# A fused recurrent attention and ELU feed-forward kernel: the lead-in, the conversion of float64 weights and the spacing of two products rearranged

**Chip, cores, metric.** One core of one Trainium2 chip. The metric is the time of one execution on the device in microseconds (us), the median of several. TensorE is called PE, its weight loads PEld, VectorE DVE, ScalarE ACT, GpSimd POOL, SyncE SP.

## The reference

A recurrent attention (per head a 48 x 48 state, decayed and updated at each step) gives x with 3072 tokens of 384 features. A feed-forward layer with ELU follows. The two weight matrices come as float64.

```python
# q, k, v, f_logit: (4 batches, 8 heads, 768 steps, 48), float32
f = 1 / (1 + exp(-f_logit))
for t in range(768):
    state = f[:, :, t, :, None] * state + einsum('bhd,bhe->bhde', k[:, :, t], v[:, :, t])
    y[:, :, t] = einsum('bhd,bhde->bhe', q[:, :, t], state)
x = y as (3072, 384)
h = x @ w_in                    # w_in  384 x 2048, float64 in DRAM
g = where(h > 0, h, exp(min(h, 0)) - 1)
out = g @ w_out                 # w_out 2048 x 384, float64 in DRAM
```

## The kernel before

The tokens go in 12 units of 256. In block m the kernel does the feed-forward layer of unit m and, in between, the attention of unit m + 1. A block has 16 places s. At even places stands an *up* product (a pair of feature tiles: 12 matmuls into `psH`), whose result goes through ACT (relu, exp) and DVE (`gg`); at odd places a *down* product of an earlier pair. `xt` is a unit's attention output, turned so that the up product can read it; `wi` (three rows kt of 2048 columns) and `wo` are the converted weights.

```python
def up(P):                                   # pair P = 8 m + j
    ph = ps.tile([128, 2, U], FP32, tag="h", bufs=2)
    for i in range(2):
        for kt in range(3):
            matmul(ph[:, i], lhsT=wi[:, kt, n : n + 128], rhs=xts[m][:, kt, :], ...)
    g = gs[P] = sb.tile([128, 2, U], FP32, tag="gg", bufs=4)
    scalar.activation(g, ph, Relu, scale=-1.0);  scalar.activation(g, g, Exp, scale=-1.0)
    vector.scalar_tensor_tensor(out=g, in0=g, scalar=-1.0, in1=ph, op0=add, op1=max)
    # ... from block 2 on: 4 sums of g for the product scheme with seven products

def attention(u):                            # places at which the pieces of unit u stand
    return {3: [transposed(u, 0), transposed(u, 1)],   # psT: k transposed
            6: [advance(u)],                 # psU: state products, then the state steps on DVE
            8: [scores(u)],                  # psS: scores, in the same two PSUM banks as psU
            10: [outputs(u)], 12: [carried(u)]}        # psY
```

A float64 word is read as two 32-bit words and rounded to float32 on the chip, 16 parts of 768 KB, all in block 0 and just before it:

```python
def rounding(n):   # ACT, in place: low word -> 0..8
    scalar.activation(raw.bitcast(I32)[:, 0::2], raw.bitcast(U32)[:, 0::2], Copy, scale=2.0**-29)
def convert(n):    # three DVE instructions
    tensor_scalar(out=bits, in0=hi, scalar1=3, scalar2=0x3FFFFFF8, op0=logical_shift_left, op1=bitwise_and)
    tensor_tensor(out=bits, in0=bits, in1=rnd, op=add)
    scalar_tensor_tensor(out=to, in0=hi, scalar=-(2**30), in1=bits, op0=bitwise_and, op1=bitwise_or)
```

The instructions of block 0 and of the lead-in keep the order of the source; after that the build's scheduler sets the order of every engine. 16 *checks* read the weights a second time and reduce them (32 reductions on DVE), to see that all lie in the range that the conversion supports. Unit 0 has code of its own before: its outputs are multiplied straight into the places of `xt` that the up product reads, while for all other units six small DMA moves inside `xt` put a part of the rows in place.

Of the kernel before, what the change touches and what calls it, by code (L numbers as in the profile page):

```python
# [8 lines left out]
FP32 = mybir.dt.float32  # L9
I32 = mybir.dt.int32  # L10
U32 = mybir.dt.uint32
AF = mybir.ActivationFunctionType
# [343 lines left out]
def fast(ctx: ExitStack, tc: tile.TileContext, q, k, v, f_logit, w_in, w_out, out, flag):  # L356
# [14 lines left out]

# [17 lines left out]
    DIRECT = 2  # L389
    AHEAD = 7  # L390
# [35 lines left out]
    start.enter_context(tc.manual_schedule())  # L426
    blank(0, nc.vector, nc.gpsimd)
    load(0, nc.scalar)

    ident = cst.tile([128, 128], FP32, name="ident")  # L430
# [14 lines left out]
    for i in range(1, NB):  # L445
        blank(i, nc.gpsimd)
    between = cst.tile([128, NW, HP], FP32, name="between")
    fine = cst.tile([128, HP, NC], FP32, name="fine")
    nc.vector.memset(fine[:], 1.0)
    py = ps.tile([128, HP, W], FP32, tag="a1", name="psY")  # L450
    nc.vector.memset(py[:], 0.0)
# [15 lines left out]
    parts = [(0, 0), *((j + i, 1 - i) for j in range(NFT // 2 - 1) for i in (1, 0)), (NFT // 2 - 1, 1)]  # L467
# [19 lines left out]
    def rounding(n):  # L487

        if wide and n < NFT:
            raw = raws[n]  # L490
            nc.scalar.activation(
                raw.bitcast(I32)[:, 0::2], raw.bitcast(U32)[:, 0::2], AF.Copy, scale=2.0**-29
            )

    def convert(n):





        if not wide or n >= NFT:
            return
        j, out_ = parts[n]
        raw = raws.pop(n)
        rnd = raw.bitcast(I32)[:, 0::2]
        hi = raw.bitcast(I32)[:, 1::2]
        bits = sb.tile([128, 2 * DM], I32, tag="bits", name=f"bits{n}", bufs=1)
        nc.vector.tensor_scalar(
            out=bits[:], in0=hi, scalar1=3, scalar2=0x3FFFFFF8,
            op0=ALU.logical_shift_left, op1=ALU.bitwise_and,  # L510
        )
        nc.vector.tensor_tensor(out=bits[:], in0=bits[:], in1=rnd, op=ALU.add)
        to = wo[:, 2 * j : 2 * j + 2] if out_ else wi[:, :, j * 256 : (j + 1) * 256]

        def rows(x):
            return x.rearrange("p (k f) -> p k f", k=to.shape[1])

        nc.vector.scalar_tensor_tensor(
            out=to.bitcast(I32), in0=rows(hi), scalar=-(2**30), in1=rows(bits[:]),
            op0=ALU.bitwise_and, op1=ALU.bitwise_or,  # L520
        )
# [19 lines left out]

    restart = cst.tile([128, HP, U], FP32, name="restart")
    nc.gpsimd.memset(restart[:], 0.0)

    def gates(u):

        f = qkf[u % NB]["f"]
        pts[u] = sb.tile([128, HP, U], FP32, tag="p", name=f"p{u}")
        for i in range(2):
            a = f[:, 2 * i : 2 * i + 2] if u else f[:, :, i * W : (i + 1) * W]  # L550
            nc.scalar.activation(a, a, AF.Exp, scale=-1.0)
            nc.scalar.activation(a, a, AF.Copy, bias=1.0)
            if u:
                nc.gpsimd.tensor_copy(restart[:, 2 * i : 2 * i + 2, ::C], a[:, :, ::C])
                nc.gpsimd.memset(a[:, :, ::C], 0.0)  # L555

    def growth(u, pairs, cols):

        t = qkf[u % NB]
        for p in range(pairs.start, pairs.stop):  # L560
            a = t["f"][:, p, cols]
            nc.vector.tensor_tensor_scan(  # L562
                out=a, data0=a, data1=restart[:, p, cols] if u else a,
                initial=1.0, op0=ALU.mult, op1=ALU.max,
            )
        k_ = t["k"][:, pairs, cols]
        nc.gpsimd.tensor_tensor(out=k_, in0=k_, in1=t["f"][:, pairs, cols], op=ALU.mult)  # L567

    def decays(u, pairs, cols):

        t = qkf[u % NB]
        nc.vector.reciprocal(pts[u][:, pairs, cols], t["f"][:, pairs, cols])  # L572
        q_ = t["q"][:, pairs, cols]
        nc.vector.tensor_tensor(out=q_, in0=q_, in1=pts[u][:, pairs, cols], op=ALU.mult)
# [7 lines left out]
    def prepare(u):  # L582

        gates(u)
        yield
        for i in range(2):
            for p in range(2 * i, 2 * i + 2):
                growth(u, slice(p, p + 1), slice(0, U))
            yield
        for p in range(HP):  # L590
            decays(u, slice(p, p + 1), slice(0, U))
            yield
        watch(u)

    def transposed(u, w, bank):

        pt = ps.tile([128, HP, 128], FP32, tag=bank, name=f"psT{u}_{w}")
        for p in range(HP):
            nc.tensor.transpose(pt[:, p, :], in_=qkf[u % NB]["k"][:, p, w * W : (w + 1) * W], identity=ident[:])  # L599
        kns[u, w] = sb.tile([128, HP, 128], FP32, tag="kn", name=f"kn{u}_{w}")  # L600
        nc.scalar.copy(kns[u, w][:], pt[:])

    def stepped(u, c, pu, end):

        s = sb.tile([128, HP, D], FP32, tag="state", name=f"state{u}_{c}", bufs=6)
        now = pu
        if u % UPB or c:
            nc.vector.tensor_tensor(out=s[:], in0=pu, in1=sts[u, c][:], op=ALU.add)
            now = s[:]
        decay = pts[u][:, :, end - 1 : end].broadcast_to([128, HP, D])  # L610
        nc.vector.tensor_tensor(out=s[:], in0=now, in1=decay, op=ALU.mult)
        sts[(u, c + 1) if end < U else (u + 1, 0)] = s

    def scores(u):
# [3 lines left out]
        pc = [ps.tile([128, NW, HP, C], FP32, tag=f"a{r}", name=f"psS{u}_{r}") for r in range(2)]  # L618
        for w in range(NW):
            for p in range(HP):  # L620
                for b in range(2):
                    cols = slice(w * W + b * C, w * W + b * C + C)
                    for r in range(2):
# [3 lines left out]
                        )  # L627
        for r in range(2):
            nc.vector.tensor_tensor(
                out=at[:, r].rearrange("k w p i -> k (w p) i"), in0=pc[r][:].rearrange("k w p i -> k (w p) i"),  # L630
# [3 lines left out]
    def advance(u):  # L634

        last = u % UPB == UPB - 1
        pu = [ps.tile([128, NW, HP, D], FP32, tag=n, name=f"psU{u}_{n}") for n in ("a0", "a1")]
        for w in range(NW):
            for p in range(HP):
                for r in range(2):  # L640
                    h = 2 * p + r
                    for b in range(2):
                        nc.tensor.matmul(  # L643
                            pu[b][FULL[r], w, p], lhsT=kns[u, w][FULL[b], p, FULL[r]],
# [3 lines left out]
        for c in range(NC - last):  # L648
            stepped(u, c, pu[c % 2][:, c // 2], (c + 1) * C)

    def outputs(u):


        pys[u] = [ps.tile([128, NW, HP, C], FP32, tag=f"a{b}", name=f"psY{u}_{b}") for b in range(2)]
# [15 lines left out]
    def carried(u):  # L670
# [17 lines left out]
        nc.scalar.copy(to[:, 0], py[0][:])  # L688
        for r in range(2):
            nc.scalar.copy(to[FULL[r], 1], py[1][FULL[1 - r]])  # L690
        for i in range(2 * NKT):
            r, j = divmod(i, NKT)
            frm, g = 64 * r + j * PAD, 64 * r + D
            nc.sync.dma_start(out=x[g : g + PAD, j, :], in_=x[frm : frm + PAD, NKT, :])

    def first_scores(w):
        t = qkf[0]
        cols = slice(w * W, (w + 1) * W)
        at = ats[0, w] = sb.tile([128, 2, HP, W], FP32, tag="at", name=f"at0_{w}")
        pc = [ps.tile([128, HP, W], FP32, tag=f"m{2 + r}", name=f"psS0_{w}_{r}") for r in range(2)]  # L700
        for p in range(HP):
            for r in range(2):
                nc.tensor.matmul(
                    pc[r][:, p], lhsT=t["k"][HALF[r], p, cols], rhs=t["q"][HALF[r], p, cols],
                    start=True, stop=True,
                )
        for r in range(2):
            nc.vector.tensor_tensor(
                out=at[:, r], in0=pc[r][:], in1=causal[:].unsqueeze(1).broadcast_to([128, HP, W]),
                op=ALU.mult,  # L710
            )

    def first_advance(w):
        pu = ps.tile([128, HP, D], FP32, tag="a0", name=f"psU0_{w}")
        for p in range(HP):
            for r in range(2):
                h = 2 * p + r
                nc.tensor.matmul(
                    pu[FULL[r], p], lhsT=kns[0, w][:, p, FULL[r]], rhs=vs[0][:, w, h * D : (h + 1) * D],
                    start=(p == 0), stop=(p == HP - 1), skip_group_check=True,  # L720
                )
        stepped(0, w, pu[:], (w + 1) * W)

    def first_outputs(w):





        cols = slice(w * W, (w + 1) * W)  # L730
        q_ = qkf[0]["q"]
        if w == 0:
            xts[0] = sb.tile([128, HP, U], FP32, tag="xt", name="xt0", bufs=3)
        at = ats.pop((0, w))
        for part in range(2 if w else 1):
            for i in range(2 * NKT):
                j, r = divmod(i, 2)
                n = slice((j - 1) * PAD, (j + 1) * PAD)
                v0 = (2 * NKT + r) * D
                nc.tensor.matmul(  # L740
                    py[64 * r + 32 : 64 * r + 64, j, :],
                    lhsT=sts[0, w][HALF[r]].rearrange("p a d -> p (a d)")[:, NKT * D + n.start : NKT * D + n.stop]
                    if part else vs[0][:, w, v0 + n.start : v0 + n.stop],
                    rhs=q_[HALF[r], NKT, cols] if part else at[:, r, NKT],
# [238 lines left out]
```

## Time and profile before

| | kernel before |
|---|---|
| median of 3 runs | 619.69 us (619.1 to 622.33) |
| span of the profiled run, granted clock | 620.9 us, 0.966 |
| first up product starts | 33.94 us |
| gg of pairs 0, 7, 14, 22 start | 39.42, 95.98, 151.91, 205.31 us |
| dense block (from transposes to transposes) | 44.87 us |

The first rows of up products on PE in order of time (start, length, line, instruction, number of matmuls merged in the row; in brackets idle time before it and what ended it).

```profile
33.94 6.74 PE L790 MATMUL psH<-xt,wi 128*128 128x256 f32 x24
...
51.55 3.80 PE L790 MATMUL psH<-xt,wi 128*128 128x256 f32 x12
```

### The profile page before, as it was taken

To read this page: it belongs to the slowest core of one execution; us is meant where nothing else is said; L and a number is where in the kernel's file an instruction comes from. 1 tells how busy PE (TensorE), PEld (TensorE's weight loads), DVE (VectorE), ACT (ScalarE), POOL (GpSimd) and SP (SyncE) were. 2 spreads that over 40 slices of the span, in tenths; PEclk is the share of its full clock that TensorE was granted. 3 is DMA by queue.
4 is the path that set the end of the run, shared out by engine and by line. 5 is a ranking of instruction groups with operands and counts; after the bars stand their busy time and mean duration, and the time that the engine had idled before them with its cause. 6 is when DMAs were issued, how large, how long until landed. Compare 5 with 4: busy or idle time off the path is not lost.

```text
span 620.9 us, 13009 instructions
## 1 busy us (share of the span) xinstructions
PE 572.7 (92%) x5402; PEld 499.3 (80%) x5402; DVE 413.4 (67%) x839; ACT 196.7 (32%) x352; POOL 59.1 (10%) x115
## 2 busy tenths in 40 slices
PE   2787699898999899999999999999999999999994
PEld 1556476675879899899999899999989989999993
DVE  6879999998699976667576675483493443532432
ACT  2254244233413323325314322323313313323220
POOL 7021003223001001002002001000000000000000
PEclk9887799979999999999999999999999999999998
DMA  8999709338682403003112112002000000000000
GB/s 187 250 253 246 184 3 197 64 84 261 221 279 79 159 32 87 26 26 86 44 28 69 41 27 59 27 26 59 25 2 8 26 2 8 26 3 8 27 0 31
DMA packets 31781, 50.78 MB, mean 82 GB/s; under 512 B 3520, under 2 KB 24544, under 8 KB 31712
## 3 DMA queue, kind: packets, MB, share of 16 engines
q1 hardware_dynamic: 31088, 49.26, 30.0%
q8 instruction: 44, 0.72, 0.5%
q10 hardware_dynamic: 624, 0.59, 0.4%
q14 instruction: 25, 0.20, 0.1%
HBM read 44.04 MB, written 4.72 MB: 79 GB/s over the span
## 4 chain that ended last, share of the span: by engine, by line
PE 69%; DVE 14%; DMA 8%; issue 5%; POOL 1%; ACT 1%; SPq 0%; DVEq 0%; POOLq 0%
PE psH L790 33%; PE psM L840 25%; DMA area<-in_moe_w_in_dram 5%; DVE p L572 4%; PE psM L818 3%; DVE f L562 3%; DMA q<-in_q_dram 2%; PE psS L624 2%; DVE spans L536 2%; PE psU_a L643 2%; DVE gg L797 2%; PE psY L661 1%; PE psT L599 1%; PE psY L681 1%; DMA f<-in_f_logit_dram 1%
## 5 line engine op out<-in xcount | busy, mean ns | idle before, releaser
L790 PE MATMUL psH<-xt,wi 128*128 128x256 f32 x1152 | 275.2, 390 | 0.0
L790 PEld LDWEIGHTS psH<-xt,wi 128*128 128x128 f32 x1152 | 218.8, 194 | 32.2
L797 DVE SCALAR_TENSOR_TENSOR gg<-gg,psH 128x512 f32<-128x512 f32 x96 | 64.8, 676 | 162.5 <-ACT gg L796 132.4
L795 ACT ACTIVATE gg<-psH 128x512 f32<-128x512 f32 x96 | 57.2, 596 | 323.6 <-PE psH L790 299.2
L840 PE MATMUL psM<-area,sums 128*128 128x192 f32 x480 | 91.3, 326 | 0.0
L572 DVE RECIPROCAL p<-f 128x256 f32<-128x256 f32 x48 | 82.5, 1734 | 0.3
L840 PEld LDWEIGHTS psM<-area,sums 128*128 128x128 f32 x480 | 80.2, 190 | 0.0
L840 PE MATMUL psM<-wo,gg 128*128 128x192 f32 x320 | 65.5, 327 | 3.5 <-DVE gg L797 3.5
L840 PEld LDWEIGHTS psM<-wo,gg 128*128 128x128 f32 x320 | 55.4, 190 | 8.3 <-DVE gg L797 4.7
L567 POOL TENSOR_TENSOR k<-k,f 128x256 f32<-128x256 f32 x48 | 39.7, 853 | 230.0 <-DMA k<-in_k_dram 196.0
L796 ACT ACTIVATE gg<-gg 128x512 f32<-128x512 f32 x96 | 60.6, 631 | 2.6
L818 PE MATMUL psM<-wo,gg 128*128 128x384 f32 x128 | 47.3, 516 | 3.3 <-DVE gg L797 3.3
L807 DVE TENSOR_TENSOR sums<-gg 128x128 f32<-128x128 f32 x160 | 42.5, 306 | 2.0
L818 PEld LDWEIGHTS psM<-wo,gg 128*128 128x128 f32 x128 | 25.3, 203 | 19.4 <-DVE gg L797 4.1
L562 DVE TENSOR_TENSOR_SCAN f<-f,restart 128x256 f32<-128x256 f32 x44 | 31.6, 761 | 11.6 <-POOL f L555 11.6
L840 PE MATMUL psM<-area,gg 128*128 128x192 f32 x160 | 39.1, 326 | 0.0
L840 PE MATMUL psM<-wo,sums 128*128 128x192 f32 x160 | 39.1, 326 | 0.0
L599 PE MATMUL psT<-ident,k 128*128 128x128 f32 x96 | 15.3, 298 | 18.3 <-POOL k L567 18.3
L536 DVE TENSOR_REDUCE spans<-area 128x1 f32<-128x768 f32 x32 | 29.3, 942 | 2.0 <-DMA area<-in_moe_w_out_dram 1.7
L599 PEld LDWEIGHTS psT<-ident,k 128*128 128x128 f32 x96 | 12.0, 151 | 21.3 <-POOL k L567 20.0
L840 PEld LDWEIGHTS psM<-area,gg 128*128 128x128 f32 x160 | 28.1, 190 | 0.1
L840 PEld LDWEIGHTS psM<-wo,sums 128*128 128x128 f32 x160 | 28.1, 190 | 0.0
(79 smaller groups left out, 427.5 us busy)
## 6 DMA issues: line engine op xcount, KB each, us to landing
area<-in_moe_w_out_dram SPq DMA_DIRECT2D x16, 768.0 KB, 7.7
area<-in_moe_w_in_dram SPq DMA_DIRECT2D x8, 768.0 KB, 5.9
v<-in_v_dram SPq DMA_DIRECT2D x12, 384.0 KB, 4.4
area<-in_moe_w_in_dram SPq DMA_DIRECT2D x16, 288.0 KB, 9.0
f<-in_f_logit_dram SPq DMA_DIRECT2D x23, 192.0 KB, 4.3
k<-in_k_dram SPq DMA_DIRECT2D x23, 192.0 KB, 3.9
q<-in_q_dram SPq DMA_DIRECT2D x23, 192.0 KB, 3.6
out_dram<-o SPq DMA_DIRECT2D x10, 384.0 KB, 2.5
```

What stands on the lines that cost most here:

```text
L536: nc.vector.tensor_reduce(out=spans[:, i, n : n + 1], in_=raw.bitcast(FP32)[:, 1::2], axis=mybir.AxisListType.X, op=op, apply_absolute_val ...
L562: nc.vector.tensor_tensor_scan(out=a, data0=a, data1=restart[:, p, cols] if u else a, initial=1.0, op0=ALU.mult, op1=ALU.max,)
L567: nc.gpsimd.tensor_tensor(out=k_, in0=k_, in1=t["f"][:, pairs, cols], op=ALU.mult)
L572: nc.vector.reciprocal(pts[u][:, pairs, cols], t["f"][:, pairs, cols])
L599: nc.tensor.transpose(pt[:, p, :], in_=qkf[u % NB]["k"][:, p, w * W : (w + 1) * W], identity=ident[:])
L790: nc.tensor.matmul(ph[:, i], lhsT=wi[:, kt, n : n + 128], rhs=xts[m][:, kt, :], start=(kt == 0), stop=(kt == NKT - 1),)
L795: nc.scalar.activation(g[:], ph[:], AF.Relu, scale=-1.0)
L796: nc.scalar.activation(g[:], g[:], AF.Exp, scale=-1.0)
L797: nc.vector.scalar_tensor_tensor(out=g[:], in0=g[:], scalar=-1.0, in1=ph[:], op0=ALU.add, op1=ALU.max)
L807: nc.vector.tensor_tensor(out=s[:, i], in0=x, in1=y, op=op)
L818: nc.tensor.matmul(pm[t][:], lhsT=g[:, i, t * 128 : (t + 1) * 128], rhs=wo[:, 2 * j + i, :], start=(j == 0 and i == 0), stop=(j == NP - 1 ...
L840: nc.tensor.matmul(pm[bank][:, half * DH : (half + 1) * DH], lhsT=x, rhs=y, start=first, stop=(j == NP - 1), skip_group_check=True,)
```

## The change

Its intent: less DVE work for the weights, a simpler lead-in (unit 0 like every other unit), PE less often waiting for gg (down two pairs behind up instead of one), the checks spread out. The core of the diff, cut:

```diff
+    LAG = 2
+    nc.scalar.preload_act_table(AF.Exp)
-    parts = [(0, 0), *((j + i, 1 - i) for j in range(NFT // 2 - 1) for i in (1, 0)), (NFT // 2 - 1, 1)]
+    parts = [(j, 0) for j in range(LAG)] + [(j + i, i == 0) for j in range(NP - LAG) for i in (LAG, 0)]
+    parts += [(j, 1) for j in range(NP - LAG, NP)]
-    def rounding(n): ...
-    def convert(n): ...
+    def split(n):
         nc.vector.tensor_scalar(out=bits[:], in0=hi, scalar1=3, scalar2=0x3FFFFFF8, ...)
+        nc.vector.tensor_scalar(out=hi, in0=hi, scalar1=-(2**30), scalar2=None, op0=ALU.bitwise_and)
+        nc.scalar.activation(raw.bitcast(U16)[:, 2::4], raw.bitcast(U32)[:, 0::2], AF.Copy, scale=2.0**-29)
+    def merge(n):
+        nc.vector.tensor_tensor(out=to.bitcast(I32), in0=rows(bits[:]), in1=rows(hi), op=ALU.add)
 ... in carried(u):
+        queues = (nc.sync,) if u else (nc.sync, nc.scalar, nc.gpsimd)
         for i in range(2 * NKT):
-            nc.sync.dma_start(out=x[g : g + PAD, j, :], in_=x[frm : frm + PAD, NKT, :])
+            queues[i % len(queues)].dma_start(out=x[g : g + PAD, j, :], in_=x[frm : frm + PAD, NKT, :])
-    def first_scores / first_advance / first_outputs ...     # unit 0's own code
 ... in attention(u):
-            3: [lambda: transposed(u, 0, "a0"), lambda: transposed(u, 1, "a1")],
-            6: [lambda: advance(u)],
-            8: [lambda: scores(u)],
+            **{p: [lambda p=p: decays(u, p)] for p in range(HP)},
+            4: [lambda: watch(u)],
+            5: [lambda: transposed(u, 0, "a0"), lambda: transposed(u, 1, "a1")],
+            7: [lambda: advance(u), *(lambda c=c: step(u, c) for c in range(NC))],
+            8: [lambda: mask(u, scores(u))],
 ... in the main loop:
-                rounding(s + 4)
-                convert(s + 3)
+                split(s + 3)
+                merge(s + 2)
-            elif P:
-                down(P - 1)
+            elif P >= LAG:
+                down(P - LAG)
-            if 4 <= m < 8 and s >= NFT - 4:
-                check(4 * (m - 4) + s - NFT + 4)
+            if 3 <= m < 11 and s in (8, 14):
+                check(2 * (m - 3) + s // 14)
```

The changed kernel also gives out each unit's output in four moves instead of one, those of the last unit partly on ACT's queue.

## The prediction

> **What bounds the kernel now.** I read the 40 slices, then the busy time of the engines stage by stage, the waits of the matmul engine (PE), VectorE's (DVE's) instructions in order of time, and the chain.
>
> First DMA and DVE in the slices of the page (15.5 us each):
>
> ```profile
> DVE  6879999998699976667576675483493443532432
> ...
> DMA  8999709338682403003112112002000000000000
> ```
>
> DMA is full for 70 us (the float64 weights), DVE is at 9 for slices 4 to 10 and 12 to 14. The stages (window, length, busy time of each engine, granted clock, DMA share, GB/s):
>
> ```profile
> 8.00:34.00 26.00, 17.68 (x145) 12.56 (x145) 21.73 (x30) 6.00 (x10) 5.55 (x7) 0.85 1.08 240
> 34.00:52.00 18.00, 11.96 (x44) 8.81 (x43) 15.46 (x21) 8.96 (x15) 6.01 (x8) 0.78 1.06 254
> 52.00:72.00 20.00, 14.97 (x116) 11.01 (x114) 19.24 (x26) 9.63 (x14) 0.00 (x0) 0.93 1.06 244
> 72.00:99.40 27.40, 26.56 (x268) 18.99 (x269) 26.04 (x45) 8.76 (x17) 1.10 (x4) 0.90 0.21 46
> 99.40:157.00 57.60, 51.66 (x418) 37.53 (x417) 54.63 (x74) 21.69 (x41) 17.55 (x32) 0.91 0.62 158
> 157.00:208.40 51.40, 48.46 (x451) 42.41 (x450) 45.02 (x82) 17.76 (x33) 4.56 (x12) 0.97 0.61 192
> 208.40:253.30 44.90, 43.57 (x464) 39.47 (x463) 33.48 (x75) 15.13 (x28) 3.96 (x8) 1.00 0.24 71
> 253.30:570.30 317.00, 316.39 (x3287) 289.90 (x3285) 177.77 (x434) 95.67 (x176) 13.24 (x24) 1.00 0.10 30
> ```
>
> DVE (the third busy time) sets the pace up to about 208 us; from 208 PE is dense and DVE works little over half the time. PE's waits after 215 us say the same:
>
> ```profile
> PE psM L840 <- DVE gg L797: 1.9, 2, 1.3
> ```
>
> So the time is "when PE becomes dense" plus PE's work after it. A dense block is 8 up products (12 records, 2.59 us), 8 down products (14 records, 2.28 us) and one unit's attention (transposes 0.9, four groups of some 1.1 us: 5.2 us): 44.2 us, and 44.87 us in the chain (from the 446.14 row to the 491.01 row):
>
> ```profile
> 446.14 2.59 PE psH L790 x12
> ...
> 491.01 2.59 PE psH L790 x12
> ```
>
> **What the skill says.** The Trainium skill, "DMA: Bandwidth & Descriptors", section "Queues, rings and completion order": an engine consumes each queue's descriptors in ring order and goes round-robin between queues. The trace agrees: the small moves of xt land in a median 1.8 us when DMA is quiet, but what the sync queue gives out in the lead-in takes 6 to 10 us, as 24.71 to 35.12 in the chain:
>
> ```profile
> 24.71 10.40 DMA area<-in_moe_w_in_dram
> 35.12 6.81 DMA area<-in_moe_w_in_dram
> ```
>
> "VectorE: DVE Perf Modes", section "Mode 2×_2P": a one-source fp32 operation in SBUF does two elements a cycle, one with two tensors one. It agrees: 768 elements take 0.61 us with one source (L508) and 0.96 us with two (L518):
>
> ```profile
> L508 DVE TENSOR_SCALAR bits<-area 128x768 int32<-128x768 int32 x16 | 9.8, 611 | 0.1
> L518 DVE SCALAR_TENSOR_TENSOR wi<-area,bits 128x768 int32<-128x768 int32 x8 | 7.7, 957 | 0.3
> ```
>
> "ScalarE: Activation LUTs", section "What ACT_TABLE_LOAD costs": 1283 ns. The trace has 1.28 us, at 5.28 us, right after the first gates land.
>
> **The change, part by part.** I add up DVE's instructions in the order in which each build gives them to DVE, at the mean durations of the groups less 0.06 to 0.08 us for overlap (reciprocal 1.67, scan 0.65, gg 0.62, check reduction 0.86, one-source weight step 0.56, byte-wise integer add 1.00, two-source step 0.97, small ones 0.2 to 0.5). I mark three points, the gg of pairs 0, 14 and 22 (a pair is two of the 16 feature tiles of a block; 8 pairs a block). For the kernel before the sums are 27.6, 136.9 and 181.8 us, and the trace has these gg at 39.42, 151.91 and 205.31 us: DVE idle of 11.8, 15.0 and 23.5 us. For the changed kernel the sums are 25.3, 144.9 and 180.8 us.
>
> Weights: 16 times (0.56 + 1.00 + 0.97) becomes 16 times (0.56 + 0.56 + 1.00): 6.6 us off DVE, all of it where DVE is the bound. ScalarE keeps its 16 steps of 0.90 us.
>
> Checks: 32 reductions of 0.86 us, the same. The source spreads them over blocks 3 to 10, but after block 0 the scheduler places instructions itself, and the build has 21 reductions ahead of the gg of pair 14 (6 before) and all 32 ahead of that of pair 18. They come earlier, not later: 15 x 0.86 = 12.9 us more ahead of pair 14. That is why its sum grows by 8.0 us although the weights give 6.6 back; the sum at pair 22 falls by 1.0 only because 5 more reductions (4.3 us) precede it.
>
> Unit 0: its score masks go from four to two (1.3 us less), its state steps from 3 to 7 before the first gg (1.3 us more), a restart memset (0.95) replaces one of psY (0.49): nothing on balance. But before, unit 0's outputs were written straight into place; now six small moves must land before the first up product, two on the sync queue. Ahead of them there stand loads of units 0 and 1 (3.14 MB) and seven weight parts (5.5 MB), 8.65 MB. At the rates above (1.3 MB by 8 us, 6.2 MB more by 34 us, then 254 GB/s) they are through at 38.3 us. The DVE chain is ready long before: first scan at some 6.2 us (7.89 before; the table load and half the first exp gone), four pairs of 2.8 us to 17.5, scores 22, masks 23.4, states 25.4, copies some 27. So the first up product starts at about 38.5 us instead of 33.94. The first gg came 5.5 us after it before, so now at 44.0; DVE's idle by then is 44.0 - 25.3 = 18.7 us against 11.8. DVE does its list strictly in order, so these 7 us eat up the 6.6 us of the weights.
>
> Down two pairs behind up: in block 0 and 1 DVE has more work than PE, so the lag gives only less idle. I take 1 us of further idle up to pair 14 (3.2 before): gg 14 at 144.9 + 18.7 + 1 = 164.6 us. From there DVE's list needs 39.9 us to the gg of pair 24 while PE has more to do, so PE is dense: 8 ups 20.7, two old downs 5.2, six new downs 13.7, one attention 5.2, plus the 0.7 us that a block measures over its sum: 45.5 us, to 210.1 us. The kernel before is in the same state (down of 22 next) at 206.03 us, and needs 414.9 us from there. The lag should remove its 1.9 us of waits for gg, and four smaller output moves on two queues some 0.7 us of the 9.4 us tail: 210.1 + 414.9 - 2.6 = 622.4 us on the profile's scale, where before has 620.9; on that of the medians 1.2 less, about 621.
>
> **The rivals.** First, the sync queue's two moves overtake the weights. The moves on the other two queues surely will, and packets of several queues interleave; against it is the 6.8 to 10.4 us in the chain for what the sync queue issued then. The first up would start at about 31.5 us, 7 us earlier: 614 to 615 us. I give this 35%.
>
> Second, DVE is no longer the bound after block 0: PE is dense from 39 us on with the lag. Up to the up of pair 24 PE has 24 x 2.59 + 16 x 2.59 + 6 x 2.28 + 3 x 5.2 = 133 us, so it would get there at 172 us instead of 206: some 585 us. Against it: DVE's sum alone at pair 14 is 144.9 us, before any idle. I give it 4%.
>
> Third, the check transfers, now up from about 105 us with the loads of four more units, hold up DVE in line: 12.6 MB of checks and 4.7 MB of loads need 69 us at 250 GB/s, and the reductions are wanted within some 75. The kernel before shows such a wait (1.7 us). If it bites: 3 to 6 us more, 625 to 628 us. 10%.
>
> **Range and chances.** 621 at nearly two thirds and 614.5 at one third give 619.0 us. Errors of 3 us each in the first up, in DVE's sum and in the idle make some 5 us, with the third rival above: 609 to 627. Faster by 2% is below 607.3 us, which even the first rival doesn't reach: 0.06. Slower by 2% is above 632.1: 0.03. Within 2%: 0.91.
>
> **What would show it.** First up product at 38 to 39 us and held by a sync-queue move of xt; first gg at 44. Weight steps of 0.61, 0.61 and 1.0 us, their sum 6 to 7 us lower. Reductions between 120 and 185 us, not spread over blocks 3 to 10. The gg of pair 14 at 162 to 168 us, PE dense from there, no wait of PE for gg after 215 us, blocks of 44.9 us. Wrong if the first up is at 33 us or earlier (first rival), if DVE has idle slices after 50 us (the order is not what binds), if the reductions wait for DMA by over 2 us (third), or if the in-place one-source step takes 0.96 us instead of 0.61 (5.6 us more on DVE).

## The result, and the profile after

The changed kernel takes 658.08 us (median of 4, 657.26 to 660.76) against 620.99 us of the kernel before in the same rounds (4 runs): **slower**, ratio 1.0607 (95% interval 1.056 to 1.0654). Ratios are the mean time of one kernel's fast runs over that of the other's of the same rounds, so they are not quite the ratio of the medians. The profiled run has a span of 655.5 us at a clock of 0.972, so its mean clock is not lower than before (0.966). It is lower from 52 to 99 us: 0.74 and 0.75, where the kernel before had 0.93 and 0.90. Whether that is only a consequence of PE's waits there was not tested by itself.

| | before | predicted | after |
|---|---|---|---|
| first up product | 33.94 | 38.5 | 49.12 |
| gg of pair 0 | 39.42 | 44.0 | 55.90 |
| gg of pair 7 | 95.98 | - | 133.36 |
| gg of pair 14 | 151.91 | 164.6 | 185.82 |
| dense block | 44.87 | 44.9 | 46.30, 45.86 |
| span | 620.9 | 622.4 | 655.5 |

DVE and DMA in the 40 slices of the page (16.4 us each here). DVE is at 6, 1, 5, 6 and 6 in slices 2 to 6, where it was at 8, 7, 9, 9 and 9 before, and DMA is not full in any slice after the third.

```profile
DVE  7615668999887846766657649448367443443432
...
DMA  9997477176672300301211201102000000000000
```

By stages (window, length, busy time of PE, PEld, DVE, ACT, POOL, clock, DMA share, GB/s), in the windows that the prediction used. From 34 to 52 us little works but DMA: PE 2.88 us instead of 11.96, DVE 1.99 instead of 15.46. From 52 to 99.4 us PE is busy 0.44 to 0.69 of the time and DVE 0.63 to 0.72, so neither is the bound there.

```profile
34.00:52.00 18.00, 2.88 (x7) 2.38 (x8) 1.99 (x3) 4.11 (x5) 0.62 (x4) 1.00 1.06 240
52.00:72.00 20.00, 8.81 (x21) 6.05 (x19) 12.69 (x18) 7.19 (x7) 1.45 (x2) 0.74 0.57 136
72.00:99.40 27.40, 18.85 (x119) 13.54 (x120) 19.84 (x34) 14.97 (x14) 1.45 (x2) 0.75 0.73 181
```

PE's waits up to 220 us (what waited, for whom: us in total, times, longest):

```profile
PE psH L718 <- DVE wi L521: 25.3, 5, 8.0
PE psH L718 <- DMA xt<-xt: 21.6, 2, 20.7
```

**The late start (second line).** The sync queue's instructions in order of time. It gives out the load of v at 24.48 us and then nothing for 7.1 us, and two moves of xt only at 39.40 us:

```profile
24.48 0.39 SPq L416 DMA_DIRECT2D v<-in_v_dram  x1
31.96 0.38 SPq L481 DMA_DIRECT2D area<-in_moe_w_out_dram  x1
...
39.40 2.07 SPq L682 DMA_DIRECT2D xt<-xt  x2
```

The chain has these waits in a row. The move that ends at 31.94 us is one of the *scalar* queue; the weight part of the sync queue starts the moment it has landed.

```profile
30.08 1.86 DMA xt<-xt
31.96 4.70 DMA area<-in_moe_w_out_dram
...
40.96 8.02 DMA xt<-xt
49.12 5.47 PE psH L718 x12
```

The list of instructions of the build tells why. All DMAs of the sync and the scalar queue take eight completion semaphores (DMAHW0 to 7) in turn in the order of the source, and each waits for the one that had its semaphore last. The two scalar-queue moves of xt took numbers 4 and 6 (the loads of unit 1, just before in the sync queue, take 3, 5, 7, 0, 1, 2 and 3 and leave these two out). So weight part 3, the next one in the sync queue, waits for number 4, a move that itself waits for the attention of unit 0 (a second build of the kernel gave the same list):

```
21 DMACopy q_72<-in_q_dram 48x4x256 [waits DMAHW1]
22 DMACopy q_72<-in_q_dram 48x4x256 [waits DMAHW2]
23 DMACopy v_78<-in_v_dram 128x2x384 [waits DMAHW3]
24 DMACopy area<-in_moe_w_out_dram 128x2x384 [waits DMAHW4]
25 DMACopy area<-in_moe_w_in_dram 48x3x256 [waits DMAHW5]
26 DMACopy area<-in_moe_w_in_dram 16x3x256 [waits DMAHW6]
```

**The merge wait (first line).** PE in order of time, up to 80 us. The up products of pairs 1 and 2 begin with the few matmuls that need not wait and then stand for 8 us, until a write of `wi` releases them. From gg to gg it takes 13.4 us (55.90, 69.32, 82.73); rows of 12 and 14 matmuls take 5.49 and 6.21 us here, where 12 take 2.59 us in the dense blocks.

```profile
49.12 6.21 PE L718 MATMUL psH<-xt,wi 128*128 128x256 f32 x14 [20.70 <-DMA xt<-xt]
63.35 5.49 PE L718 MATMUL psH<-xt,wi 128*128 128x256 f32 x12 [8.03 <-DVE wi L521]
76.77 4.63 PE L718 MATMUL psH<-xt,wi 128*128 128x256 f32 x10 [7.93 <-DVE wi L521]
```

In the build's list the first matmul of such a product (kt = 0) has no such wait, the second (kt = 1) has one. The merge that stands ahead of it in the source writes other columns: those of the pair two further on, but in all three rows kt. In a second build the wait of pair 1's second matmul is for the addition that writes columns 768 to 1023, those of pair 3. A range from its first to its last element covers the columns of rows 1 and 2 that this product reads, but not those of row 0, which fits. In the kernel before, the last conversion step had the same place and the same output, and its products have no such wait: there it was an ordinary two-source instruction, now it is an integer addition that the trace shows as a custom one. So gg of a pair comes before the merges on DVE, the merges before the next up product on PE, that before ACT, and ACT before the next gg: a loop with no overlap.

**Longer blocks.** After 215 us PE no longer waits for gg, as predicted, but the blocks take 46.30 us. What PE waits for there is the state steps:

```profile
PE psS L610 <- DVE state L594: 3.2, 10, 0.6
```

The scores write the banks from which the state steps read. In the chain (258.47 us) the last state step stands right before the scores, which then take 1.93 us instead of about 1.1:

```profile
258.47 0.37 DVE state L594
258.84 0.14 issue
258.98 1.93 PE psS L610 x62
```

**ACT's weight step** is twice as long (groups of the two kernels; the last numbers are busy us, mean ns and idle time before):

```profile
L491 ACT ACTIVATE area<-area 128x768 int32<-128x768 uint32 x16 | 13.7, 903 | 0.0
```

```profile
L507 ACT ACTIVATE area<-area 128x768 uint16<-128x768 uint32 x16 | 30.6, 1926 | 29.6 <-DVE area L506 27.3
```

The rest went as intended: DVE is busy for 402.6 us instead of 413.4, and from the last matmul to the end it takes 7.1 us instead of 9.1.

### The profile page after: what moved, and what is told of

Its sections match the earlier page's. It is cut to its first block, busy times and chain, and to the rows that moved or that the text cites. A ratio compares the mean times of both kernels' runs of the same rounds, so it can differ in the third digit from the quotient of the medians.

```text
span 655.5 us, 13271 instructions
## 1 busy us (share of the span) xinstructions
PE 572.8 (87%) x5506; PEld 499.8 (76%) x5506; DVE 402.6 (61%) x840; ACT 214.4 (33%) x360; POOL 57.1 (9%) x120
## 4 chain that ended last, share of the span: by engine, by line
PE 72%; DVE 15%; DMA 5%; ACT 4%; issue 3%; SPq 0%; POOL 0%; DVEq 0%; POOLq 0%
PE psH L718 37%; PE psM L768 25%; PE psS L610 3%; PE psM L746 2%; DMA q<-in_q_dram 2%; DVE p L564 2%; DVE f L561 2%; PE psY L647 2%; PE psY L667 2%; DMA xt<-xt 2%; DVE gg L725 1%; DVE state L594 1%; PE psT L579 1%; ACT gg L723 1%; ACT gg L724 1%
## 5 line engine op out<-in xcount | busy, mean ns | idle before, releaser
L718 PE MATMUL psH<-xt,wi 128*128 128x256 f32 x1152 | 282.6, 395 | 46.9 <-DVE wi L521 25.3
L718 PEld LDWEIGHTS psH<-xt,wi 128*128 128x128 f32 x1152 | 221.8, 197 | 83.2 <-DVE wi L521 27.8
L566 POOL TENSOR_TENSOR k<-k,f 128x256 f32<-128x256 f32 x48 | 36.9, 789 | 283.7 <-DMA k<-in_k_dram 176.3
L768 PEld LDWEIGHTS psM<-wo,gg 128*128 128x128 f32 x320 | 54.9, 190 | 3.6
L735 DVE TENSOR_TENSOR sums<-gg 128x128 f32<-128x128 f32 x160 | 44.4, 318 | 1.7
L746 PE MATMUL psM<-wo,gg 128*128 128x384 f32 x128 | 44.9, 494 | 0.0
L507 ACT ACTIVATE area<-area 128x768 uint16<-128x768 uint32 x16 | 30.6, 1926 | 29.6 <-DVE area L506 27.3
L746 PEld LDWEIGHTS psM<-wo,gg 128*128 128x128 f32 x128 | 24.4, 193 | 14.0 <-issue 0.6
L610 PEld LDWEIGHTS psS<-q,k 48*64 48x64 f32 x768 | 20.1, 146 | 15.5 <-DVE state L594 9.0
L610 PE MATMUL psS<-q,k 48*64 48x64 f32 x768 | 22.5, 234 | 10.2 <-DVE state L594 9.9
```

The costliest lines, as they stand in the source:

```text
L507: nc.scalar.activation(raw.bitcast(U16)[:, 2::4], raw.bitcast(U32)[:, 0::2], AF.Copy, scale=2.0**-29)
L566: e.tensor_tensor(out=x[:, p], in0=x[:, p], in1=y, op=ALU.mult)
L610: nc.tensor.matmul(pc[r][FULL[b], w, p], lhsT=t["k"][HALF[r], p, cols], rhs=t["q"][HALF[r], p, cols], start=True, stop=True,)
L718: nc.tensor.matmul(ph[:, i], lhsT=wi[:, kt, n : n + 128], rhs=xts[m][:, kt, :], start=(kt == 0), stop=(kt == NKT - 1),)
L735: nc.vector.tensor_tensor(out=s[:, i], in0=x, in1=y, op=op)
L746: nc.tensor.matmul(pm[t][:], lhsT=g[:, i, t * 128 : (t + 1) * 128], rhs=wo[:, 2 * j + i, :], start=(j == 0 and i == 0), stop=(j == NP - 1 ...
```

## The experiments

Theory: three separate causes, the late start, the merge wait and the place of the state products. The rival all along: DVE's list sets the pace up to 205 us, as I had predicted, and waits of PE there cost nothing. Twelve kernels were run. All gave correct results. They ran in three groups, each beside the kernel before on the same chip; its medians were 622.14, 620.25 and 623.31 us, so across groups I compare the ratios to the kernel before.

| kernel | median us | ratio to before (95%) | first up | gg 0 | gg 7 | gg 14 | gg 22 |
|---|---|---|---|---|---|---|---|
| changed | 658.08 | 1.0607 (1.056-1.0654) | 49.12 | 55.90 | 133.36 | 185.82 | 235.04 |
| e1_rows | 647.97 | 1.0424 (1.0356-1.0492) | 49.07 | 55.84 | 119.02 | 173.04 | 224.31 |
| e1b_upfirst | 646.67 | 1.0382 (1.0322-1.0442) | 49.62 | 56.20 | 119.37 | 173.50 | 221.38 |
| e2_moves_pool | 642.56 | 1.0332 (1.0267-1.0397) | 40.34 | 46.28 | 120.76 | 170.93 | 215.68 |
| e2b_moves_sync | 653.01 | 1.0493 (1.0428-1.0559) | 43.32 | 50.11 | 124.46 | 180.85 | 228.97 |
| e3_both | 636.19 | 1.0232 (1.0158-1.0305) | 41.26 | 48.05 | 111.40 | 161.88 | 211.25 |
| e4_early | 626.50 | 1.0098 (1.0054-1.0141) | 40.18 | 46.29 | 108.08 | 160.29 | 210.58 |
| e6_moves_first | 629.41 | 1.0131 (1.0094-1.0168) | 34.90 | 41.07 | 106.11 | 156.71 | 205.79 |
| e7_checks_held | 631.23 | 1.0164 (1.0128-1.0199) | 40.62 | 47.27 | 111.85 | 157.68 | 209.24 |
| e8_all | 615.38 | 0.9923 (0.9886-0.9960) | 34.44 | 40.40 | 103.32 | 151.96 | 199.27 |
| e9_three_mends | 621.43 | 0.9979 (0.9935-1.0023) | 34.46 | 40.11 | 103.89 | 156.07 | 207.58 |
| e10_lag1 | 623.65 | 1.0011 (0.9966-1.0056) | 34.36 | 40.91 | 102.93 | 151.32 | 200.65 |
| b1_held | 621.01 | 0.9990 (0.9940-1.0040) | 32.53 | 39.53 | 96.53 | 148.53 | 196.44 |

### e1_rows: the merge written as three additions

```diff
-        nc.vector.tensor_tensor(out=to.bitcast(I32), in0=rows(bits[:]), in1=rows(hi), op=ALU.add)
+        for i in range(1 if out_ else NKT):
+            r = slice(0, 2) if out_ else slice(i, i + 1)
+            nc.vector.tensor_tensor(
+                out=to[:, r].bitcast(I32), in0=rows(bits[:])[:, r], in1=rows(hi)[:, r], op=ALU.add)
```

> Edit: the changed kernel, with the merge of an up weight written as three additions (one for each of the three 128-row parts) instead of one that spans all three. Theory (merge wait): the up products of block 0 wait for a merge whose columns they don't read, because one addition over three rows of wi counts as the whole range between its first and last element; three additions don't. Then the 25.3 us of PE waits on the merges fall below 8 us, the step from gg to gg in block 0 falls from 13.4 us to 9 to 11 us, and the time by 9 to 17 us, to 641 to 649 us. First up product unchanged at 49 us. Rival (late start only): the products truly need these merges, or DVE's list alone sets the pace; then the time stays at 657 to 661 us.

Measured: 647.97 us, the waits on merges are gone, and the step from gg to gg is 10.3 us (55.84, 66.18, 76.48). PE's longest waits up to 220 us:

```profile
PE psT L583 <- POOL k L570: 27.4, 6, 15.3
PE psH L722 <- DMA xt<-xt: 20.8, 2, 20.5
```

The merge wait was real and costs 1.8% (10 us by the medians). But 25.3 us of waits became 10: once PE ran on, it met the transposes of the next unit, which wait for k, which waits for DVE's decays between the weight steps. From here on DVE's list does set the pace of block 0.

### e1b_upfirst: the same wait taken away by order

```diff
+            P = m * NP + s // 2
+            if m == 0 and s % 2 == 0:
+                up(P)              # matmuls only; relu, exp and gg stay where they were
             if m == 0:
                 split(s + 3)
                 merge(s + 2)
```

> Edit: the changed kernel with its single merge over three rows, but in block 0 the matmuls of an up product stand in the source ahead of the split and merge of the same place instead of after them; the order on VectorE and ScalarE is as it was. Second test of the merge wait with other means: if the up products wait for a merge only since it stands before them in the source and counts as a write of the whole range, then moving them before it helps as much as the three additions did in e1_rows (647.97 us): 645 to 650 us. If the three additions helped for another reason (other timing on VectorE, other placement by the scheduler of what comes after block 0), the time stays at 655 us or more.

Measured: 646.67 us, as with the three additions. Of the 25.3 us of waits on `wi` 8.0 are left here, none in e1_rows. Two edits that share nothing but the removed wait give the same gain within the noise, so the wait is the cause, not a side effect of other timing. That the build takes the addition's output as one range is what fits both. It is seen in the waits that the build sets; the addition itself names three separate pieces of 512 16-bit words as its output, so the range is an affair of the build and not of the instruction.

### e2_moves_pool and e2b_moves_sync: where unit 0's moves are given out

```diff
-        queues = (nc.sync,) if u else (nc.sync, nc.scalar, nc.gpsimd)
+        queues = (nc.sync,) if u else (nc.gpsimd,)       # e2b_moves_sync: (nc.sync,) for all
```

> Edit: the changed kernel, with all six moves of xt of unit 0 given out by GpSimd's queue. Theory (late start): the first up product at 49.1 us waits for two moves on the sync queue that stand behind weights, and the sync queue itself stood still for 7.1 us for the moves on the scalar queue. With the moves on GpSimd the sync queue issues weight part 3 before 28 us, the first up product starts at 31 to 35 us, its gg at 38 to 42 us (55.9 in the changed kernel), and the time falls by 12 to 16 us to 642 to 647 us, as all after it moves with it. Rival (the merge wait is all that counts, DVE's list or the weights set the pace): the first up comes early but the gg of pair 7 stays near 133 us and the time at 655 us or more.

> Edit: the changed kernel, with all six moves of xt of unit 0 on the sync queue. It splits the late start into its two parts: the stall of the sync queue (7.1 us, for completion semaphores held by the scalar queue's moves) is gone, but the moves still stand behind the weights. If the stall is the larger part, weight part 3 is issued by 28 us and the first up product starts at 40 to 43 us, time 650 to 653 us. If only the place behind the weights counts, the first up product stays at 47 us or later, time 656 us or more.

Measured: 642.56 us with GpSimd, 653.01 us with sync. In both, weight part 3 is given out at 22.7 us instead of 31.96. The first time is within what I gave, the second at its upper edge (653; its first up product is 0.3 us after the 43 us that I gave). So the late start costs 2.75 points (hundredths of the time of the kernel before) as far as this edit cures it, of which the stall of the sync queue is 1.1. But in e2_moves_pool the first up product starts at 40.34 us, not at 31 to 35. The moves on GpSimd's queue, with nothing of their own ahead of them, took 7.4 us to land (the last line of the view of xt up to 60 us, for e2_moves_pool and for the changed kernel):

```profile
DMA to landing us min/median/max: 7.3/7.4/7.7
```

```profile
DMA to landing us min/median/max: 1.8/1.9/9.4
```

So the 1.9 us of the scalar and GpSimd moves in the changed kernel was an accident of the stall: DMA had run dry (share 0.50 from 28 to 32 us). The Trainium skill, "DMA: Bandwidth & Descriptors", section "Queues, rings and completion order", says that a completion increment lands only after every earlier write from that DMA engine, across its queues. The run fits this: an empty queue does not overtake the weights (7.4 us). It does not tell whether the data or the increment was late.

### e3_both: merges by rows and moves on GpSimd

> Edit: both, merges by rows and all moves of unit 0 on GpSimd's queue. If late start and merge wait are two separate causes that add up, 37 us of the loss over the kernel before are about accounted for: first up at 31 to 35 us, gg of pair 14 at 155 to 163 us (151.9 in the kernel before, 185.8 in the changed one), time 624 to 634 us, with what remains being the longer blocks (1 us each). If they overlap, it is no better than the better of the two alone: 641 us or more.

Measured: 636.19 us, 2 us above what I gave. The gains are 1.8 and 2.75% alone and 3.75% together: nearly additive, less 0.8 points of overlap. The first up product is at 41.26 us for the reason just found.

### e4_early: the state products one place earlier (on e3_both)

```diff
-            7: [lambda: advance(u), *(lambda c=c: step(u, c) for c in range(NC))],
+            6: [lambda: advance(u), *(lambda c=c: step(u, c) for c in range(NC))],
```

> Edit: as e3_both, and the state products and steps of the next unit one place earlier in the source (place 6 instead of 7, the scores stay at 8), as the kernel before had it. Theory: the blocks of some 46 us (44.9 in the kernel before) are longer because the scores' banks are released only by the last state step on VectorE, which has one place less of time. Then the period falls by 0.5 to 1 us, the wait of the scores for the state steps (0.6 us a time after 215 us) goes, and the time falls by 4 to 9 us against e3_both, to 627 to 632 us. Rival: the period comes from something else (the lag, other order of the down products); then it stays at 636 us within 1.5.

Measured: 626.50 us, 0.5 us below what I gave for it, and 1.3% (9.7 us by the medians) below e3_both. Transposes of two blocks in the chain and the scores between them, first of e3_both (46.30 us apart), then of e4_early (44.89 us, as in the kernel before):

```profile
226.89 0.87 PE psT L583 x8
...
237.18 1.94 PE psS L614 x62
...
273.19 0.87 PE psT L583 x8
```

```profile
226.39 0.87 PE psT L583 x8
...
235.68 1.09 PE psS L614 x64
...
271.28 0.87 PE psT L583 x8
```

PE has no wait at all after 215 us in e4_early. The wait view had shown only 3.2 us for this cause; the other part was inside the scores, which run as slowly as the banks come free (some 1.93 us for 1.09, 0.84 us a block). With 0.84 us in each of the eight blocks after 215 us that have scores, and the 3.2 us of waits, that makes 9.9 us.

### e6_moves_first: weights held back for unit 0's moves (on e3_both)

```diff
-    for n in range(AHEAD):
+    for n in range(4):
         fetch(n)
 ...
     carried(0)                 # moves on the sync queue
+    for n in range(4, AHEAD):
+        fetch(n)
```

> Edit: as e3_both, but the six moves of unit 0 are on the sync queue and stand there ahead of weight parts 4 to 6, which are given out only after them. In e3_both the moves on GpSimd's queue took 7.8 us to land although nothing stood before them in their queue, since all 16 engines were busy with weights; in the changed kernel those on the scalar and GpSimd queues took 1.9 us, while the sync queue stood still. Theory: what the moves wait for is the weights in flight on the same engines. With fewer weights in flight they land in 2 to 3 us, the first up product starts at 33 to 37 us (41.3 in e3_both), and the time falls by 3 to 7 us against e3_both, to 629 to 633 us. Rival: the weights, held back, then arrive later and VectorE waits for them; the first up comes early, the gg of pair 7 stays at 111 us, and the time at 635 us or more.

Measured: 629.41 us, 1.0% below e3_both. The moves land in 1.8 us and the first up product starts at 34.90 us:

```profile
DMA to landing us min/median/max: 1.7/1.8/1.9
```

The edit differs from e3_both in the queue as well; but on the sync queue without the hold (e2b_moves_sync) the moves took 2.5 to 8.1 us, so it is the hold that counts. The gg of pair 7 comes 5.3 us earlier too, so the weights that were held back were not missed. With this, unit 0 starts nearly as early as with the code of its own that it had before.

### e7_checks_held: the checks made late (on e3_both)

```diff
-                check(2 * (m - 3) + s // 14)
+                check(2 * (m - 3) + s // 14, gs[P])
 ... in check:
+        nc.gpsimd.tensor_copy(raw.bitcast(FP32)[:, 0:1], after[:, 0, 0:1])
         nc.sync.dma_start(out=raw, in_=flat[n // 2])
```

> Edit: as e3_both, and each check's transfer is made to wait for the gg of the pair at which the source places it (one element copied into its buffer first), so that the checks really are spread over blocks 3 to 10. It tests the reason that I gave for what sets the pace up to 205 us: VectorE's list. Theory: 31 reductions of some 0.86 us leave the part in which VectorE is the bound (up to the gg of pair 22) and run where it works a little over half the time; the gg of pair 22 comes 15 to 25 us earlier than the 211.3 us of e3_both, the time falls by 10 to 24 us, to 612 to 626 us. Rival: the matmul engine and its waits (for k, for the scores) set the pace there, or the late reductions hold up gg in the dense blocks: time 630 us or more.

Measured: 631.23 us, 0.7% below e3_both (a difference that the two intervals do not clear): the theory fell, and the time is just inside the rival's range. In the build no reduction is left ahead of the gg of pair 26, where e3_both had 31 ahead of pair 22, and still that gg came only 2.0 us earlier (that of pair 26 4.3 us, the end 2.8 us). The stretch from 162 to 211 us, e3_both and then e7_checks_held (columns as in the stages above): DVE falls from 44.33 to 27.14 us, PE goes from 47.11 to 48.60 of 49 us.

```profile
162.00:211.00 49.00, 47.11 (x432) 39.45 (x432) 44.33 (x77) 15.63 (x29) 4.15 (x8) 0.97 0.69 227
```

```profile
162.00:211.00 49.00, 48.60 (x455) 41.64 (x454) 27.14 (x56) 15.91 (x30) 4.15 (x8) 1.00 0.17 44
```

So in these two kernels DVE was not what bound that stretch: PE was as full. It is otherwise once the three mends are in: from e9_three_mends to e8_all (below) the same edit takes PE from 45.34 to 49.00 us in that stretch and brings the gg of pair 22 8.3 us earlier. The run also bounds a side effect of e1 to e3: they moved reductions, too (21 ahead of pair 14 in the changed kernel, 12 in e1_rows, 10 in e2_moves_pool, 8 in e3_both, by the build's order, as the scheduler answers to any edit). Taking away all of them is worth 0.7% in e3_both, so those shifts can hardly carry the 1.8 and 2.75%.

### e8_all and e9_three_mends: everything together

e8_all is e6_moves_first with the edits of e4_early and e7_checks_held; e9_three_mends is the same without the hold of the checks.

> Edit: all of these at once (merges by rows, moves of unit 0 first on the sync queue, state products one place earlier, checks held). If the causes are separate their gains add: some 603 to 615 us, below the kernel before. If they overlap (each frees VectorE or the matmul engine only until the next bound), no better than the best of the three by more than 3 us.

> Edit: the changed kernel with the three mends (merges by rows, moves of unit 0 on the sync queue ahead of weight parts 4 to 6, state products one place earlier) and nothing else; the checks lie as the scheduler places them. If the loss of the changed kernel is these three causes and no other, they bring it to the time of the kernel before: 658.1 less 21.9 (merges and late start as far as GpSimd's queue cures it), less 9.7 (state products), less 6.8 (moves first) is 619.7 us, so 617 to 623 us, within 0.5% of the kernel before. If there is a fourth cause, or they overlap, 625 us or more; if the rest of the change was worth something and the mends uncover it, 614 us or less.

Measured: 621.43 us with the three mends, ratio 0.9979 with an interval that holds 1: the three causes make up the net loss within 0.4%. Other parts of the change may still give and take inside that. The steps add up as well: from 1.0607, 3.75 points by e3, 1.34 by e4 and 1.01 by e6 leave 0.9997. The lead-in is still 2.3 us behind the kernel before at the gg of pair 22. From pair 48 on the gg of both come at the same times (within 0.1 us), but with the lag of two one more down product (2.28 us) is then still to do; the tail after the last matmul, 2.0 us shorter, makes up for it.

With the checks held as well, 615.38 us, ratio 0.9923 (interval 0.9886 to 0.996): the best of all kernels here, somewhat faster than both the changed kernel and the one before, though less than 1%, and 0.4 us above the range that I gave.

### b1_held and e10_lag1: what late checks and the lag are worth

b1_held is the kernel before with the spread and the hold of the checks alone; e10_lag1 is e8_all with `LAG = 1`.

> Edit: the kernel before, with only the spread of the checks over blocks 3 to 10 and the hold that makes it real (one element of a gg copied into the buffer ahead of each transfer). It tells whether late checks are worth as much without the rest of the change, and whether it beats the mended kernel with all of it (e8_all, 615.4 us). VectorE has 27 fewer reductions ahead of the gg of pair 22, some 23 us of work; but in e7_checks_held only 5 us of that came through, as the matmul engine was the next bound. Expectation: 614 to 618 us; if the matmul engine's waits for gg in blocks 1 and 2 (3.8 us) are all that it can win, not less than 616 us. If the late reductions disturb the dense blocks: 621 us or more.

> Edit: e8_all with down one pair behind up again instead of two (which also brings the down weights forward by one part). It tells what the lag is worth. If the lag gives what I predicted, no more wait of the matmul engine for gg in the dense part and less in blocks 0 to 2, this is 2 to 5 us slower than e8_all's 615.4 us: 617 to 620 us. If the lag is worth nothing once the state products are in place: 614 to 617 us.

Measured: b1_held 621.01 us, ratio 0.9990, the case in which late reductions disturb the dense blocks: no gain to be seen, though its gg of pair 22 comes 8.9 us earlier than before (196.44 us). e10_lag1 623.65 us, ratio 1.0011 against 0.9923 of e8_all (another group, so compared by ratio): with checks held the lag is worth 0.9%, more than I gave here and more than the 2 us of the prediction. PE's waits after 220 us in e10_lag1 (e8_all has none for gg there):

```profile
PE psM L773 <- DVE gg L730: 5.0, 3, 2.7
PE psM L773 <- ACT gg L728: 1.0, 3, 0.4
PE psM L773 <- DVE u L783: 0.7, 2, 0.4
```

In e10_lag1 a block takes 46.89 us (216.33 to 263.22 us in the chain), in b1_held 47.3 and 46.0 us (from 253.50 and 300.82 us). Late reductions stand ahead of a gg on DVE now and then; with down one pair behind up PE then stops, with two pairs it has another product to do. The gg times fit this: the 8.9 us that b1_held is ahead at pair 22 shrink to 2.2 us in the span (618.7 against 620.9), while the 8.3 us of e8_all over e9_three_mends stay (612.6 against 621.1). So the hold gives little without the lag, and the lag is what lets the spread of the checks pay. What the lag gives without the hold was not run on the mended kernel.

## Why the prediction was wrong

The range was 609 to 627 us and the time is 658. On the profile's scale the miss is 33.1 us (622.4 to 655.5): 21.2 us up to the gg of pair 14, the rest after it. My sum for that gg was 144.9 us of DVE's list and 19.7 us of idle. The trace has 138.5 us of busy DVE (the third busy time below) and so 47.4 us of idle: the list was even shorter than I had summed, and the step that failed is the idle, what DVE waits for. After it, the longer blocks are some 10 us (e4).

```profile
0.00:185.82 185.82, 114.13 (x1066) 82.82 (x1067) 138.47 (x211) 77.48 (x107) 34.71 (x80) 0.91 0.70 172
```

- **First up product at 38.5 us: failed, 49.12.** I had taken the queues as rings that only share bandwidth, added up the bytes ahead of the moves, and left out that an issue can wait. The shared completion semaphores tied the sync queue to the scalar queue (7.1 us), and two moves then took a further 8 us behind weights (e2, e2b). The two loads that I showed for the skill's account of the queues say that a transfer takes longer when DMA is full; they do not say when an issue may start.
- **Rival 1, an up product at 31.5 us: not reached by any run.** I was sure that the moves on the other two queues overtake the weights. In these runs they did so only with few weights in flight (7.4 us against 1.8, e2 and e6).
- **"1 us of further idle up to pair 14": failed.** I looked at what a merge costs (0.95 us, right) and not at who waits for it. The merge wait alone was 25.3 us of PE's time and 1.8% of the whole (e1, e1b). The waits of the changed build's up products on `wi` could have been read beforehand; I read its order on DVE only.
- **"A dense block stays at 44.87 us": failed, 46.30 and 45.86.** The diff moves the state products from place 6 to 7 and leaves the scores at 8. I counted the instructions, which are the same, and not the distance to the one that waits for them (e4: 1.3%).
- **"DVE's list sets the pace up to 205 us": half right.** It does so in block 0 (e1: 10.3 us a pair, DVE dense). From 111 us on it is not the only bound: 27 us of reductions out of the way gave 0.7% (e7), but 8.3 us at the gg of pair 22 with the three mends in (e8, e9). The table in the prediction shows it already: PE is busy 26.56 of 27.40 us and 48.46 of 51.40 us in stages that I gave to DVE alone. So my weight for every us on DVE was too high, and the 6.6 us that the new weight steps save may not have come through whole (not shown). In the changed kernel DVE is at 5 and 6 in the slices from 49 to 98 us, the sign that I had named for an order that does not bind. (A slip: in the slices before, DVE is at 9 in 4 to 9; slice 10 is an 8.)
- **ScalarE keeps its 0.90 us: failed, 1.93.** The Trainium skill, "ScalarE: Activation LUTs", section "What ACT_TABLE_LOAD costs", gives 186 ns + 0.833 ns an element, 826 ns for 768 elements (an estimate from the page). The 32-bit step agrees to within 10% (903 ns), the one that writes 16-bit halves does not. What it costs the whole was not run apart; e9_three_mends has it and is level with the kernel before, so it is hidden or balanced by the other parts.
- **Rival 3, reductions that wait for DMA:** they waited 2.4 us in all, just over the 2 us that I had named as its sign, and little beside the miss.
- **Right:** the weight steps on DVE (0.56, 0.55 and 0.95 us), the reductions early and not spread (from 146 to 203 us), no wait of PE for gg after 215 us, and a gain in the tail (2.0 us where I had 0.7).

Not settled: what the new weight steps are worth by themselves; they were run only with the other parts.

## What to carry to other kernels

When an instruction is replaced by another with the same output, read who waits for it in the new build, not only what it costs: here the wider dependence cost 25.3 us of waits, the instruction 0.95 us. Before a producer is moved in the order of an engine that runs in order, count the distance to its next consumer on the other engine; one place less cost about a microsecond in every dense block here. And a gain of one part may only show once another is in place (checks held: nothing on the kernel before, 0.6%, just at the edge of the noise, from e9_three_mends to e8_all, where the lag is), while a small transfer that many wait for should be given out before the large ones, not on another queue.

## What the Trainium skill lacked or had wrong

- "DMA: Bandwidth & Descriptors", section "Queues, rings and completion order", tells how queues share engines, but not that two queues can be tied together on the issuing side by completion semaphores that they share: here DMAs of the sync and the scalar queue took eight completion semaphores in turn, and the sync queue gave out nothing from 24.87 to 31.96 us, until a move of the scalar queue had landed. (That the sharing comes from the build, not the chip, no page says either.)
- The same section has no number for a small transfer on an otherwise empty queue beside a full one: 16 KB took 7.4 us on GpSimd's queue with weights in flight, 1.8 us on the sync queue without.
- "ScalarE: Activation LUTs" gives one throughput for every function and for fp32 and bf16; 768 elements written as uint16, one in four, took 1926 ns, as int32, one in two, 903 ns.
- No page says that the integer addition, which the trace shows as a custom DVE instruction, is ordered by the build by a wider range than an ordinary one (an inference from the waits): as one addition over three rows of `wi` it cost 25.3 us of PE's waits, as three additions none.
